# A second fold of the Fourier columns, with some moves, an order and an output tile changed

## The chip, the cores and the metric

The kernel runs on one core of a Trainium2 chip. The metric is the time of one execution on the device in microseconds (us), as the median of several runs. The engines are TensorE (PE; its weight loads appear as PEld), VectorE (DVE), ScalarE (ACT), GpSimd (POOL) and SyncE (SP), which only issues transfers (DMAs) here.

## The reference

Three stages follow each other, on 2 batches of 768 tokens. All arrays are fp32.

```
# attention: 2 batches, 8 heads, 768 tokens, 64 per head
bits   = (q @ proj > 0), (k @ proj > 0)          # 6 bits for each token
mask   = bucket(q bits) == bucket(k bits)
scores = where(mask, q @ k.T / 8, -1e9)
x      = softmax(scores) @ v                      # heads side by side: 2 x 768 x 512

# Fourier mixing over tokens and columns, then a channel MLP of width 2048
u  = x + real(fft(fft(x, axis=1), axis=2))
x  = u + relu(layernorm(u) @ w_ch1) @ w_ch2

# gated MLP: width 1024, gate mixed over tokens
h  = gelu(x @ w_in); a, v = halves of h
v  = w_sg @ (layernorm(v) * g_ln) + b_sg
out = x + (a * v) @ w_out
```

## The kernel before

Products are held to fp32 accuracy by splitting each operand into a high and a low float16 part and adding three matmuls (the pairs in `HH`: high by high, high by low, low by high); the scores of attention use fp32r parts instead. Tokens are kept in a mirrored order, so that token t and token 768 - t lie in partner tiles (tile t and tile t + 3 of the six tiles of 128 tokens).

**Attention.** For each of the 96 tiles of queries (16 heads, 6 tiles each): scores on PE, the row maximum on DVE, the exponential on ACT, a float16 split on ACT or POOL and POOL, a transpose by DMA (or, for some tiles, on PE), and the product with v on PE. `stacks` prepares a head: it makes scaled q1 and its residual k2 from one load, and then four moves of 64 partitions by 768 bring halves of q1, k1, q2, k2 where they belong; `mv` names the engine of each (S is a DMA issued by SP). Head 0 has its own list, `ENG0`. `one_hot` then writes codes into the other halves of q1 and k1.

**Fourier stage** (`fft`, once for each batch). The transform over tokens and columns is real and is folded first: rows by A + B and A - B of partner tiles (`fe`, `fo`), then columns by adding (even part) or subtracting (odd part) column c and column 512 - c. The folded parts, 257 and 256 columns wide, are split into float16 (`ee`, `oo`; the single row `oe`, `oeh`). `step1` multiplies them with the token tables (`cs`, `sn`, 385 columns) to give `yc`, `ys` and one middle row `y2`. `step2` multiplies these with the column tables (`cl`, `sl`, 257 columns), two blocks of 128 each, giving the cosine part p and the sine part q of each tile, and p - q and p + q are added to the partner tiles. `step2` runs 6 matmuls, and 2 more with `rl` where `extra` is set, 257 columns wide each, into neighbouring columns of one PSUM bank. `norm` then normalises each tile (`un`; `UN` names the engine for each batch), splits it and transposes it by DMA into `unT`.

**Channel MLP** (`ch`: lines 764 and 785 are its two products) and **gated MLP** (`gmlp`: line 881 the first product, 933 the token mixing, 984 the output product in `go`). A gated tile is turned by DMA into `gT`; `GV` lists, by count, those that take their room from the larger pool `vg` (18 buffers), the others take one of 4. `go` adds the output product to x on DVE and stores 256 KB for each of the 12 tiles.

**Order.** The two batches overlap: the second batch's attention runs beside the first batch's Fourier stage (called fft0 here) and channel MLP and beside the preparation of the weights; the second Fourier stage (fft1) runs beside the end of the first batch's channel MLP. The order in which each engine issues its instructions is made when the kernel is built, by the class `Order`: a list planner with costs for each instruction that takes, on each engine, the ready step of lowest rank. `SHIFT` adds an offset in us to the rank of named streams of work (a lower one comes earlier): w1a to w2b are weights, att1h7 is head 7 of the second batch, ch1 the second batch's channel MLP, pre1h3 the preparation that runs during head 3.

## Time and profile before

| what | value |
|---|---|
| median of 3 runs | 665.83 us (662.92 to 667.2) |
| the profiled execution | 667.98 us |
| its span, first to last instruction | 666.2 us |
| PE busy | 604.4 us of the span |
| DVE, ACT, POOL busy | 495.1, 362.2, 284.9 us |
| mean granted clock of PE | 0.967 |

The span is what the profile's rows are placed in; 1.8 us of the execution lie outside it. A row of a timeline has the start, the duration, the engine, the line of the kernel, the operation, the tile written and the tiles read. A busy time counts overlapping instructions of one engine once, and a single matmul's duration holds its latency, so the pace of matmuls is read from their starts.

### The profile page before, as it was taken

To read this page: it belongs to the slowest core of one execution; us is meant where nothing else is said; L and a number is where in the kernel's file an instruction comes from. 1 tells how busy PE (TensorE), PEld (TensorE's weight loads), DVE (VectorE), ACT (ScalarE), POOL (GpSimd) and SP (SyncE) were. 2 spreads that over 40 slices of the span, in tenths; PEclk is the share of its full clock that TensorE was granted. 3 is DMA by queue.
4 is the path that set the end of the run, shared out by engine and by line. 5 is a ranking of instruction groups with operands and counts; after the bars stand their busy time and mean duration, and the time that the engine had idled before them with its cause. 6 is when DMAs were issued, how large, how long until landed. Compare 5 with 4: busy or idle time off the path is not lost.

```text
span 666.2 us, 12742 instructions
## 1 busy us (share of the span) xinstructions
PE 604.4 (91%) x4901; PEld 412.4 (62%) x4901; DVE 495.1 (74%) x1061; ACT 362.2 (54%) x574; POOL 284.9 (43%) x246
## 2 busy tenths in 40 slices
PE   4789889847866999999999998999999999999997
PEld 3688778734755676777776647676666444444443
DVE  6897886588987866998767498669552477598883
ACT  5899999864687756675553224234352176334110
POOL 2566667594667652445424041500010004446762
PEclk9799999978968999999999999999999999999999
DMA  8999999997999999897663047942000022001335
GB/s 338 241 174 215 223 187 191 237 270 178 216 202 240 236 223 215 204 193 169 133 99 114 1 63 141 226 124 99 33 0 1 17 48 49 1 16 32 79 102 151
DMA packets 183884, 94.60 MB, mean 142 GB/s; under 512 B 166480, under 2 KB 167120, under 8 KB 183312
## 3 DMA queue, kind: packets, MB, share of 16 engines
q1 hardware_dynamic: 183392, 93.72, 64.5%
q8 instruction: 38, 0.62, 0.4%
q14 instruction: 22, 0.18, 0.1%
q10 hardware_dynamic: 432, 0.07, 0.1%
HBM read 39.31 MB, written 3.15 MB: 64 GB/s over the span
## 4 chain that ended last, share of the span: by engine, by line
PE 61%; DMA 12%; DVE 9%; ACT 7%; POOL 6%; issue 4%; SPq 1%; POOLq 0%; ACTq 0%; DVEq 0%
PE c L785 16%; PE c L764 14%; PE gi L881 9%; PE p L933 6%; DMA et<-eh 5%; PE go L984 5%; PE s L480 4%; POOL eh L347 3%; DVE nm L490 2%; PE y L635 2%; DMA k<-q 2%; DMA wide<-w 1%; DMA unT<-hl 1%; ACT e L492 1%; POOL eh L342 1%
## 5 line engine op out<-in xcount | busy, mean ns | idle before, releaser
L347 POOL TENSOR_TENSOR eh<-e,eh 128x768 f16<-128x768 f32 x80 | 138.0, 1728 | 95.9 <-ACT eh L340 93.7
L764 PE MATMUL c<-unT,w 128*128 128x256 f16 x1152 | 134.6, 273 | 4.6 <-DVE h L773 2.7
L785 PE MATMUL c<-w,h 128*128 128x512 f16 x576 | 130.9, 379 | 0.0
L764 PEld LDWEIGHTS <-w 128*128 128x128 f16 x1152 | 111.5, 98 | 25.6 <-issue 8.5
L480 PE MATMUL s<-k,q 128*128 128x384 f32 x384 | 98.5, 386 | 26.2 <-ACT e L492 15.6
L490 DVE TENSOR_REDUCE nm<-s 128x1 f32<-128x768 f32 x96 | 90.7, 949 | 22.4 <-PE s L480 20.5
L492 ACT ACTIVATE e<-s,nm 128x768 f32<-128x768 f32 x96 | 85.1, 897 | 31.2 <-DVE nm L490 20.1
L785 PEld LDWEIGHTS <-h 128*128 128x128 f16 x576 | 55.3, 98 | 59.7 <-issue 0.6
L480 PEld LDWEIGHTS s<-k,q 128*128 128x128 f32 x384 | 70.1, 208 | 33.2 <-ACT e L492 19.0
L548 PE MATMUL pav<-V,et 128*128 128x65 f16 x480 | 54.9, 198 | 12.0 <-DMA et<-eh 10.7
L772 ACT ACTIVATE h<-c 128x256 f16<-128x256 f32 x96 | 35.0, 378 | 55.4 <-PE c L764 51.8
L773 DVE SCALAR_TENSOR_TENSOR h<-c,h 128x256 f16<-128x256 f32 x96 | 39.1, 418 | 34.9 <-ACT h L772 34.8
L548 PEld LDWEIGHTS <-et 128*128 128x128 f16 x480 | 46.0, 102 | 21.5 <-DMA et<-eh 14.6
L549 PE MATMUL pav<-V,et 128*128 128x64 f16 x480 | 54.4, 196 | 0.0
L550 PE MATMUL pav<-V,et 128*128 128x65 f16 x480 | 54.3, 198 | 0.0
L881 PE MATMUL gi<-in,xT 128*128 128x512 f16 x216 | 50.5, 379 | 0.0
L881 PEld LDWEIGHTS <-xT 128*128 128x128 f16 x288 | 28.2, 98 | 34.6 <-issue 0.9
L549 PEld LDWEIGHTS <-et 128*128 128x128 f16 x480 | 46.0, 100 | 0.8
L550 PEld LDWEIGHTS <-et 128*128 128x128 f16 x480 | 46.0, 100 | 0.0
L342 POOL TENSOR_SCALAR eh<-e 128x768 f16<-128x768 f32 x32 | 30.3, 948 | 32.8 <-ACT e L492 31.0
L340 ACT ACTIVATE eh<-e 128x768 f16<-128x768 f32 x48 | 40.3, 840 | 4.2 <-DMA et<-eh 3.8
L347 POOL TENSOR_TENSOR v<-gv,v 128x512 f16<-128x512 f32 x6 | 7.3, 1238 | 57.3 <-ACT v L868 57.3
(247 smaller groups left out, 1062.6 us busy)
## 6 DMA issues: line engine op xcount, KB each, us to landing
wide<-w SPq DMA_DIRECT2D x24, 512.0 KB, 4.8
x<-qk SPq DMA_DIRECT2D x16, 384.0 KB, 4.2
k<-q SPq DMA_DIRECT2D x30, 192.0 KB, 3.8
wide<-w SPq DMA_DIRECT2D x4, 1024.0 KB, 9.3
wide<-w_in SPq DMA_DIRECT2D x16, 256.0 KB, 2.9
vst<-v SPq DMA_DIRECT2D x8, 396.0 KB, 5.0
y<-ot SPq DMA_DIRECT2D x12, 256.0 KB, 2.0
q<-q SPq DMA_DIRECT2D x15, 192.0 KB, 3.9
```

The source lines that it names most:

```text
L340: self.nc.scalar.activation(out, src, AF.Copy, scale=scale)
L347: (self.nc.vector if eng == "D" else self.nc.gpsimd).tensor_tensor(out=out, in0=a, in1=b, op=ALU.subtract)
L480: nc.tensor.matmul(s[:, hf, 0:HS], q[:, qs], k[:, hf * HS:(hf + 1) * HS], start=n == 0, stop=n == len(pairs) - 1)
L490: nc.vector.tensor_reduce(nm, x["s"], axis=AX.XY, op=ALU.max, negate=True)
L492: nc.scalar.activation(e.rearrange("p (a c) -> p a c", a=2), x["s"], AF.Exp, bias=nm)
L548: nc.tensor.matmul(pv[:, qt, 0:65], et[:, kb, :], V[:, hl, kb, 64:129], start=kb == 0, stop=False)
L549: nc.tensor.matmul(pv[:, qt, 0:64], et[:, kb, :], V[:, hl, kb, 0:64], start=False, stop=False)
L550: nc.tensor.matmul(pv[:, qt, 0:65], et[:, NT + kb, :], V[:, hl, kb, 64:129], start=False, stop=kb == NT - 1)
L764: nc.tensor.matmul(ps[:, 0:step], w1[kc][:, a, fo], uT[:, 4 * u + kc, o * P:o * P + step], start=m == 0, stop=m == 11)
L785: nc.tensor.matmul(ps, hs[n, half, f][:, a, j * P:(j + 1) * P], wv[:, w, :], start=f + m == 0, stop=f == NF - 1 and m == 2)
L881: nc.tensor.matmul(ps, xT[:, 4 * a + kc, :], w_in[kc][:, w, half * DM:(half + 1) * DM], start=n == 0, stop=n == 11)
L933: nc.tensor.matmul(ps, W[a][k][:, w, t * P:(t + 1) * P], V[v][k][:, x, :], start=n == 0, stop=n == 8)
```

## The change

The columns are folded a second time: of the 257 folded columns c, column c and column 256 - c are added and subtracted (`quarter`), because output columns of even number need only the sums and those of odd number only the differences (the other way round for the sine part). Sums and differences are written into the free half of the same tile, so the split and `step1` work on as many columns as before. `step2` then runs, for even outputs, on one block with a table of 129 columns, and for odd outputs on the other block with 128, and writes each into every second column of the PSUM tile. The number of matmuls stays, the width halves, and so do the tables `cl` and `sl`. The two fillings with zero (`oeh`, `y2`) go, because their matmuls read one row.

Head 0's four moves go to ACT, POOL, DVE, DVE in place of ACT, POOL, POOL, ACT, and the fourth reads k1's copy instead of q1. The last output tile is made, added and stored in two halves of 256 columns. `UN`, `GV`, `SHIFT` and the scale `YS` have new values.

```
 NL = DM // 2 + 1
+NE = DM // 4 + 1
 BIG = 2.0 ** 100
...
 SCALE = 1.0 / math.sqrt(D)
-YS = 2.0 ** -4
+YS = 2.0 ** -5
...
 AVL = 3
-UN = ('A', 'D')
+UN = ('D', 'A')
 LN1 = (True, False)
...
 XTB = 6
+FO = ('P', 'P')
 GOB = 2
 LO = 'PPDPDD'
-GV = (5, 8, 11)
+GV = (8, 11)
 SQ = S // 4
...
 CP = (False, False)
-ENG0 = {'hi': 'D', 'mv': 'APPA', 'oh': 'A'}
+ENG0 = {'hi': 'D', 'mv': 'APDD', 'oh': 'A'}
 W_ATT0 = 1.5
...
-    def sub(self, eng, out, a, b):
-        (self.nc.vector if eng == "D" else self.nc.gpsimd).tensor_tensor(out=out, in0=a, in1=b, op=ALU.subtract)
+    def sub(self, eng, out, a, b, op=ALU.subtract):
+        (self.nc.vector if eng == "D" else self.nc.gpsimd).tensor_tensor(out=out, in0=a, in1=b, op=op)
...
             (tk1[0:64], tq2[64:128], tq2[0:64], tk2[0:64]),
-            (tq1[64:128], tq1[0:64], tk2[0:64], tq1[64:128]),
+            (tq1[64:128], tq1[0:64], tk2[0:64], tk1[0:64] if eng is ENG0 else tq1[64:128]),
         ):
...
         sn = fp.tile([P, HT, 2, NK], F16, tag="sn", name="sn")
-        cl = fp.tile([P, 2, 2, NL], F16, tag="k1", name="cl", bufs=2)
-        sl = fp.tile([P, 2, 2, NL], F16, tag="k1", name="sl", bufs=2)
+        cl = fp.tile([P, 2, NL], F16, tag="k1", name="cl", bufs=2)
+        sl = fp.tile([P, 2, NL], F16, tag="k1", name="sl", bufs=2)
         rk = fp.tile([P, NK], F16, tag="rk", name="rk")
-        rl = fp.tile([P, NL], F16, tag="rl", name="rl")
+        rl = fp.tile([P, NE], F16, tag="rl", name="rl")
         for t, nm in ((cs, "cos_s"), (sn, "sin_s"), (cl, "cos_c"), (sl, "sin_c"), (rk, "row_k"), (rl, "row_l")):
...
         y2 = fp.tile([P, 2, NK], F16, tag="y2", name="y2")
-        nc.gpsimd.memset(oeh, 0.0)
-        nc.gpsimd.memset(y2, 0.0)
         yield 0.1
...
         oo = fp.tile([P, HT, 2, h], F16, tag="k3", name="oo", bufs=2)
-        oe = fp.tile([1, NL], F32, tag="row", name="oe")
+        oe = fp.tile([1, DM], F32, tag="row", name="oe")
+        r = h // 2
+
+        def quarter(eng, x, z):
+
+            self.sub(eng, x[:, h + 1:h + r + 1 - z], x[:, z:r], x[:, h - z:r:-1])
+            self.sub(eng, x[:, r + 1:h + 1 - z], x[:, r + 1:h + 1 - z], x[:, z:r][:, ::-1], ALU.add)
+
         for t in range(HT):
...
             nc.vector.tensor_tensor(out=e[:, 1:h], in0=e[:, 1:h], in1=e[:, DM - 1:h:-1], op=ALU.add)
-            nc.scalar.activation(ee[:, t, 0], e[:, 0:NL], AF.Copy, scale=i)
-            nc.vector.scalar_tensor_tensor(out=ee[:, t, 1], in0=e[:, 0:NL], scalar=i, in1=ee[:, t, 0], op0=ALU.mult, op1=ALU.subtract)
+            quarter("D", e, 0)
+            nc.scalar.activation(ee[:, t, 0], e[:, r:r + NL], AF.Copy, scale=i)
+            nc.vector.scalar_tensor_tensor(out=ee[:, t, 1], in0=e[:, r:r + NL], scalar=i, in1=ee[:, t, 0], op0=ALU.mult, op1=ALU.subtract)
             if t == 0:
...
                 nc.vector.tensor_copy(oe[:, h:h + 1], o[0:1, h:h + 1])
-                nc.scalar.activation(oeh[0:1, 0], oe, AF.Copy, scale=i[0:1])
-                nc.vector.scalar_tensor_tensor(out=oeh[0:1, 1], in0=oe, scalar=i[0:1], in1=oeh[0:1, 0], op0=ALU.mult, op1=ALU.subtract)
+                quarter("D", oe, 0)
+                nc.scalar.activation(oeh[0:1, 0], oe[:, r:r + NL], AF.Copy, scale=i[0:1])
+                nc.vector.scalar_tensor_tensor(out=oeh[0:1, 1], in0=oe[:, r:r + NL], scalar=i[0:1], in1=oeh[0:1, 0], op0=ALU.mult, op1=ALU.subtract)
             nc.gpsimd.tensor_tensor(out=o[:, 1:h], in0=o[:, 1:h], in1=o[:, DM - 1:h:-1], op=ALU.subtract)
-            nc.scalar.activation(oo[:, t, 0], o[:, 0:h], AF.Copy, scale=i)
-            nc.vector.scalar_tensor_tensor(out=oo[:, t, 1], in0=o[:, 0:h], scalar=i, in1=oo[:, t, 0], op0=ALU.mult, op1=ALU.subtract)
+            quarter(FO[b], o, 1)
+            nc.scalar.activation(oo[:, t, 0], o[:, r:r + h], AF.Copy, scale=i)
+            nc.vector.scalar_tensor_tensor(out=oo[:, t, 1], in0=o[:, r:r + h], scalar=i, in1=oo[:, t, 0], op0=ALU.mult, op1=ALU.subtract)
             yield 2.0
...
                 for a in range(2):
-                    nc.tensor.matmul(y[0:m, 0:NK], oeh[:, a, c0:c0 + m], rk, start=False, stop=n == last)
+                    nc.tensor.matmul(y[0:m, 0:NK], oeh[0:1, a, c0:c0 + m], rk[0:1], start=False, stop=n == last)
                     n += 1
...
         for c in range(2):
-            step1(c * P, P, ee, cs, True, yc[c])
+            step1(c * P + 1, P, ee, cs, True, yc[c])
             yield 1.9
-        step1(2 * P, 1, ee, cs, True, y2)
+        step1(0, 1, ee, cs, True, y2)
         yield 1.9
...
             p = self.pp.tile([P, 512], F32, tag="p", name="p")
-            n = 0
-            last = 5 + (2 if extra else 0)
-            for c in range(2):
+            for l in range(2):
+                n = 0
+                last = 2 + (2 if extra and not l else 0)
+                o = p[0:m, l:NL:2]
                 for a, w in HH:
-                    nc.tensor.matmul(p[0:m, 0:NL], y[c][:, a, k0:k0 + m], tab[:, c, w, :], start=n == 0, stop=n == last)
+                    nc.tensor.matmul(o, y[l][:, a, k0:k0 + m], tab[:, w, NE * l:NE + l * (NE - 1)], start=n == 0, stop=n == last)
                     n += 1
-            if extra:
-                for a in range(2):
-                    nc.tensor.matmul(p[0:m, 0:NL], y2[:, a, k0:k0 + m], rl, start=False, stop=n == last)
+                for a in range(2 if extra and not l else 0):
+                    nc.tensor.matmul(o, y2[0:1, a, k0:k0 + m], rl[0:1], start=False, stop=n == last)
                     n += 1
...
             p = step2(t * P, P, yc, cl, True)
-            q = step2(t * P, P, ys, sl, False)
+            q = step2(t * P, P, ys[::-1], sl, False)
             qdu = fp.tile([P, 3, NL], F32, tag="k3", name="qdu", bufs=2)
...
-        def go(b, t):
+        def go(b, t, parts=1):
             gT, os_ = sv.pop((b, t))
-            po = self.pc.tile([P, 512], F32, tag="go", name="go")
-            n = 0
-            for kc in range(4):
-                for a, w in HH:
-                    wv = w_out[kc // 2].rearrange("p t (k c) -> p t k c", k=2)[:, w, kc % 2, :]
-                    nc.tensor.matmul(po, gT[:, 4 * a + kc, :], wv, start=n == 0, stop=n == 11)
-                    n += 1
             ot = self.gp2.tile([P, DM], F32, tag="ot", name="ot", bufs=2)
-            nc.vector.scalar_tensor_tensor(out=ot, in0=po, scalar=os_, in1=self.XU[b][:, t], op0=ALU.mult, op1=ALU.add)
-            nc.sync.dma_start(out=self.out[b, t], in_=ot)
+            m = DM // parts
+            for j in range(parts):
+                po = self.pc.tile([P, 512], F32, tag="go", name="go")[:, 0:m]
+                c = slice(j * m, j * m + m)
+                n = 0
+                for kc in range(4):
+                    for a, w in HH:
+                        wv = w_out[kc // 2].rearrange("p t (k c) -> p t k c", k=2)[:, w, kc % 2, c]
+                        nc.tensor.matmul(po, gT[:, 4 * a + kc, :], wv, start=n == 0, stop=n == 11)
+                        n += 1
+                nc.vector.scalar_tensor_tensor(out=ot[:, c], in0=po, scalar=os_, in1=self.XU[b][:, t, c], op0=ALU.mult, op1=ALU.add)
+                nc.sync.dma_start(out=self.out[b, t, :, c], in_=ot[:, c])
...
         for x in pend:
-            go(*x)
+            go(*x, 2 if x == pend[-1] else 1)
...
     GAP = {"DVE": 0.19, "POOL": 0.13}
-    SHIFT = {"sg": 34.0, "w2a": 34.0, "fft0": -30.0, "w2b": 8.0, "out": -4.0, "fft1": -8.0, "att1h7": 4.0, "in": 4.0, "ch1": 19.0}
+    SHIFT = {"sg": 34.0, "w2a": 26.0, "fft0": -30.0, "out": -4.0, "fft1": -4.0, "att1h7": 8.0, "in": 4.0, "att1h5": 8.0, "w2b": 15.0, "ch1a": -30.0, "att1h4": 15.0, "pre1h3": -30.0}
     LOOK, OVER = 12, 0.3
...
     sn[:, [0, HS]] = 0.0
-    c = np.arange(DM // 2)
-    l = np.arange(NL)
-    a = 2 * np.pi * ((c[:, None] * l[None, :]) % DM) / DM
-    cl, sl = np.cos(a), np.sin(a)
-    sl[0] = 0.0
-    sl[:, [0, NL - 1]] = 0.0
+    c = np.arange(P)
+    le, lo = np.arange(0, NL, 2), np.arange(1, NL, 2)
+
+    def turn(f, c, l):
+        return f(2 * np.pi * ((c[:, None] * l[None, :]) % DM) / DM)
+
+    cl = np.concatenate([turn(np.cos, P - 1 - c, le), turn(np.cos, c, lo)], 1)
+    sl = np.concatenate([turn(np.sin, c, le), turn(np.sin, P - c, lo)], 1)
+    sl[0, 0:NE] = 0.0
+    sl[:, [0, NE - 1]] = 0.0
...
     rk[0] = (k % 2 == 1)
-    rl = np.zeros((P, NL), np.float16)
-    rl[0] = np.where(l % 2 == 0, 1.0, -1.0)
+    rl = np.zeros((P, NE), np.float16)
+    rl[0] = np.where(np.arange(NE) % 2 == 0, 1.0, -1.0)
     codes = np.zeros((P, 4, GH, P), np.float16)
...
     return {
-        "cos_s": lay(cs), "sin_s": lay(sn), "cos_c": lay(cl), "sin_c": lay(sl), "row_k": rk, "row_l": rl,
+        "cos_s": lay(cs), "sin_s": lay(sn), "cos_c": lay(cl)[:, 0].copy(), "sin_c": lay(sl)[:, 0].copy(), "row_k": rk, "row_l": rl,
         "codes": codes, "pops": pops, "ident": np.eye(P, dtype=np.float32),
```

## Rows read from the trace of the kernel before

**Rows 1.** The page's busy time of each engine over the whole span.

```profile
PE 604.4 (91%) x4901; PEld 412.4 (62%) x4901; DVE 495.1 (74%) x1061; ACT 362.2 (54%) x574; POOL 284.9 (43%) x246
```

**Rows 2.** Stretches: length, busy PE, PEld, DVE, ACT, POOL; granted clock, DMA share, GB/s.

```profile
0.00:16.00 16.00, 6.82 (x33) 5.25 (x34) 10.84 (x19) 9.04 (x13) 3.97 (x17) 1.00 0.85 338
133.00:167.00 34.00, 21.36 (x183) 14.02 (x183) 28.57 (x42) 19.88 (x32) 23.52 (x20) 0.80 0.95 223
167.00:216.00 49.00, 35.33 (x392) 28.56 (x392) 41.81 (x96) 37.53 (x57) 32.37 (x29) 0.79 1.09 220
...
360.00:400.00 40.00, 40.00 (x245) 23.17 (x243) 28.68 (x95) 11.56 (x26) 11.18 (x12) 1.00 0.21 34
400.00:641.00 241.00, 237.87 (x1386) 135.33 (x1385) 166.04 (x454) 89.81 (x165) 63.94 (x57) 1.00 0.27 63
641.00:666.20 25.20, 21.49 (x100) 9.54 (x98) 13.29 (x31) 1.89 (x3) 9.54 (x9) 1.00 0.47 135
```

**Rows 3.** Timeline of the first 14 us: start, duration, engine, line, operation.

```profile
5.29 1.02 DVE L354 SCALAR_TENSOR_TENSOR k<-x,qsc,q 128x768 fp32r<-128x768 f32 x1
5.35 1.65 POOL L342 TENSOR_SCALAR q<-q 64x768 fp32r<-64x768 f32 x1 [4.14 <-DVE q L344]
...
6.96 0.80 PE L446 MATMUL ct<-bits,codes 128*128 128x192 f16 x4 [0.60 <-ACT bits L400]
...
8.12 0.84 ACT L340 ACTIVATE k<-q 64x768 fp32r<-64x768 f32 x1 [1.21 <-POOL q L342]
...
9.86 0.90 ACT L370 ACTIVATE q<-ct,pops 64x768 fp32r<-64x768 f32 x1
...
11.71 5.49 PE L480 MATMUL s<-k,q 128*128 128x384 f32 x16 [3.95 <-ACT k L372]
```

**Rows 4.** Timeline of DVE in the first batch's fold.

```profile
142.25 0.41 DVE L615 TENSOR_TENSOR fe<-fe 128x255 f32<-128x255 f32 x1
...
142.65 0.67 DVE L613 TENSOR_TENSOR fe<-xu 128x512 f32<-128x512 f32 x1
```

**Rows 5.** Groups by line and shape: count, busy us, mean ns, idle before.

```profile
L773 DVE SCALAR_TENSOR_TENSOR h<-c,h 128x256 f16<-128x256 f32 x96 | 39.1, 418 | 34.9 <-ACT h L772 34.8
...
L624 POOL TENSOR_TENSOR fo<-fo 128x255 f32<-128x255 f32 x6 | 6.3, 1055 | 0.4 <-DVE oe L620 0.4
...
L615 DVE TENSOR_TENSOR fe<-fe 128x255 f32<-128x255 f32 x6 | 4.9, 813 | 0.0
L734 ACT ACTIVATE un<-xu,lnm,ln 128x512 f32<-128x512 f32 x6 | 4.8, 801 | 0.0
...
L736 DVE TENSOR_SCALAR un<-xu,mv,ln 128x512 f32<-128x512 f32 x6 | 3.5, 584 | 0.1
```

**Rows 6.** Chain of waits in the first Fourier stage: start, us, what.

```profile
135.32 0.53 POOL oeh L601
...
136.59 3.46 DVE fe L613 x2
...
157.38 2.78 PE y L635 x9
...
167.18 0.76 PE p L661 x6
```

**Rows 7.** Timeline of PE in the second Fourier stage.

```profile
377.14 0.83 PE L661 MATMUL p<-sl,ys 128*128 128x257 f16 x6
377.80 0.83 PE L661 MATMUL p<-cl,yc 128*128 128x257 f16 x6
```

**Rows 8.** Chain of waits: an attention matmul of 65 columns.

```profile
126.00 0.03 PE pav L550
```

**Rows 9.** Timeline of DVE at the end.

```profile
662.53 0.75 DVE L987 SCALAR_TENSOR_TENSOR ot<-go,os,xu 128x512 f32<-128x512 f32 x1 [1.84 <-PE go L984]
```

**Rows 10.** DMA issues by line: count, KB each, median us to landing.

```profile
y<-ot SPq DMA_DIRECT2D x12, 256.0 KB, 2.0
...
cl<-cos_c SPq DMA_DIRECT2D x2, 257.0 KB, 5.7
```

## Prediction

> **What bounds the kernel now.** I read the busy totals first: TensorE (PE) is busy 604.4 of 666.2 us, so 61.8 us of idle is all that order and latency can give back, and the rest falls only if matmuls get fewer or narrower [rows 1]. The stretches then show where that idle lies [rows 2]; subtract PE's busy time from each length. From 0 to 16 it is 9.2 us. From 133 to 216, where the first batch's Fourier stage (fft0) meets the second batch's attention, it is 12.6 + 13.7 = 26.3 us, at a granted clock of 0.80 and 0.79 (a mix of the levels 1.2 and 2.4 GHz), while VectorE (DVE) is busy 28.57 of 34 and 41.81 of 49 us. From 360 to 400, where the second Fourier stage (fft1) runs, PE has no idle at all; from 400 to 641 it has 3.1 us, in the tail 3.7. What is left, 19.5 us, lies between these, most of it in the attention before 133. So one rule for each edit: behind 216 a matmul column saved is time saved, and work added to DVE, ScalarE (ACT) or GpSimd (POOL) is covered by PE; ahead of 216 it is the other way, the latency of DVE and POOL counts and PE has room.
>
> **The start.** Head 0's first score matmul begins at 11.71 [rows 3]. Before it ACT moves one half, POOL makes two moves one after the other (the first 5.35 to 7.00), ACT the fourth move (8.12 to 8.96), then, behind a move for head 1, the two one-hots from 9.86 on, 0.9 us each. The fourth move reads the half of q1 that the first one-hot overwrites, so the one-hot must wait. After the change it reads k1's copy, and ACT has no second move. The code products end at 6.96 + 0.80 = 7.76; one-hots from 7.8 to 9.6; first score at about 9.65, which is 2.1 us earlier. The two moves on DVE start after the residual (5.29 + 1.02 = 6.31) and are shorter than it at the same 768 columns, so they end by 6.31 + 2 x 1.02 = 8.4, in time. They are queued ahead of head 1's scaling and residual on DVE, whose products are needed only after six tiles of head 0; POOL only loses work. But DVE gets up to 2 us more, and weight work behind it is pushed towards the first row maxima. I take -1.5, bounds -2.1 and 0.
>
> **Second fold, the inputs (fft0).** Each batch adds 6 DVE operations of 128 columns, 2 on one row of the odd part, and 6 on POOL of 127 columns; two POOL clears go. A clean DVE operation took 0.41 us at 255 columns and 0.67 at 512 [rows 4], so about 0.27 at 128; the same operation at 255 averaged 0.813, and POOL's 1.055, since they wait for each other there [rows 5]. So DVE pays 8 x 0.27 = 2.2 to 8 x 0.81 = 6.5, POOL 6 x 0.5 (half of 1.055) = 3.2 to 6.3, in part at the same time, and the clears come off (the first is 0.53 us of the chain, just ahead of the fold, and I put both at 1.0) [rows 6]. The chain of waits runs through DVE's fold from 136.59 up to the first Fourier matmul at 157.38 [rows 6]: none of this is hidden. I take 8 x 0.45 - 1.0 = +2.6, nearer the clean rows since narrow operations meet fewer others; bounds +0.5 and +11.8 (6.5 + 6.3 - 1.0).
>
> **Second fold, the matmuls.** The second Fourier step has 50 matmuls of 257 columns a batch (8 for the middle row, 14 for each of three tiles), and afterwards 50 of 129 or 128. Six of 257 took 377.80 - 377.14 = 0.66 us, 0.110 each [rows 7]; those of 65 columns in attention follow each other at 0.03 [rows 8]. Between the two, 129 columns give 0.057. So 50 x 0.053 = 2.7 us a batch. In fft1 PE is full, so all of it counts: -2.7. In fft0 the chain passes through these products from 167.18 with four sixes and two pairs of them, about 3.2 us, and half of that goes: -1.6, bounds -2.7 and 0.
>
> What no row shows is the place they are written to: every second column of PSUM. All matmuls in this trace write neighbouring columns. The Trainium skill, page SBUF — State Buffer, section Door 1: The DMA port swizzle, says that PSUM has lines of 8 bytes, two fp32 values, and that any access which isn't contiguous significantly slows down matmuls; a step of two columns is such an access. No run here shows it yet; it is a rival below. The page TensorE: Matmul & The Clock Gate, section Back-to-back issue gap, gives 81 ns per matmul of 128 columns with its weight load; the trace's 65-column matmuls, each with a load, run at 30 ns [rows 8], so the measurement speaks against it. By the page the saving would be 50 x 0.029 = 1.5 us a batch, and the sum 2.0 us higher (1.2 in fft1, 0.8 in fft0).
>
> **Normalisation swapped.** Batch 0's six go from ACT (0.801 us each) to DVE (0.584), batch 1's the other way [rows 5]. In 167 to 216 ACT is busy 37.53 and DVE 41.81 of 49 us [rows 2]: DVE is the fuller, yet each of the six is 0.22 us shorter. I take -0.5, bounds -1.5 and +1.5 (half of 6 x 0.584 unhidden). In fft1 the swap costs 6 x 0.22 = 1.3 us at most, hidden by PE's full queue: 0.
>
> **Fold in fft1.** The same 14 operations lie beside a PE without idle; the matmuls of the first batch's channel mixing cover them, and could be drawn forward. 0; without the cover up to +3, as in fft0.
>
> **Tail and tables.** The last output add runs from 662.53, 0.75 us for 512 columns [rows 9]; with 256 the nearest DVE row is 0.418 [rows 5], so -0.33. 256 KB took 2.0 us to land [rows 10]; half of it saves between 0 and 1.0, I take 0.3. PE's second half adds next to nothing. One more store on SP has nothing behind it. Together -0.6. The two column tables shrink from 257 KB [rows 10] to half, on a DMA system busy 0.95 in 133 to 167 [rows 2]: -0.3, bounds -1 and 0. The new scale, and loads of one row in place of 128, cost nothing: as many columns pass.
>
> **Order.** New priorities, and the fifth gated tile's transpose drawn from four buffers in place of 18: a wait there would sit on SP's queue ahead of the next transposes, with seven finished tiles pending for PE as cover (0 to +2). Priorities change no work, only idle. I take 0, bounds -7 (a quarter of the 26.3) and +4.
>
> **Sum.** -1.5 + 2.6 - 2.7 - 1.6 - 0.5 - 0.6 - 0.3 = -4.6 us. The profiled execution took 667.98, 2.15 above the median, and would come to 663.4; from the median 665.83 it is 661.
>
> **Rivals.** Strided writes cost double: if a written column takes the place of two, 129 columns need the 0.110 us of 257, both matmul terms vanish, and the time is 661 + 4.3 = 665.3. For it: the rule above; against it: nothing in the trace, either way.
> The new order is what matters: it starts attention and channel mixing so that a quarter of the 26.3 us closes, 661 - 6.6 = 654.4. For it: granted clocks of 0.8 mean that closing gaps also makes matmuls faster; against it: DVE's 84 and 85% there, which no order changes.
> Slower: DVE and POOL block each other in the fold. Each added operation then costs its blocked row and none overlap: +11.8 in place of +2.6, 670.2. The other terms give 7.2, so it ends slower than before from (7.2 + 1.0) / 14 = 0.6 us for each added operation end to end, and slower by over 1% (672.5) from 1.06, a little above the blocked means. For it: the mean of 0.813 against the clean 0.41; against it: the two engines also work side by side, and only fft0 is exposed.
> That the start doesn't move, because DVE's weight work is still ahead of the first maximum, gives 662.5 and lies within the forecast.
>
> **How the numbers follow.** Forecast 0.36, of which a quarter lies under 659.2; strided writes 0.24; order 0.28, nearly all under 659.2; blocking 0.12, two thirds over 672.5. One per cent, 6.7 us, is about what can be told from no change: three runs spread over 4.3. Faster 0.35, same 0.57, slower 0.08. The range reaches from 653 (the order rival with the start's full 2.1 and some tail) to 668 (strided writes and 2.7 more for the fold), which leaves out the blocking case and some of the luckiest orders.
>
> **What would show it.** The first score matmul near 9.65. In fft1, matmuls of 128 columns starting 0.057 apart: right; 0.110: the strided rival. DVE's fold operations of 128 columns near 0.3 or near 0.8, and the first Fourier matmul 20 us after the fold begins, or 23 or more. PE's idle in 133 to 216 against 26.3. The forecast is wrong if PE idles in fft1's stretch, or if that idle moves by more than 5 us either way.

## The result and the profile after

After the change the kernel took 669.28 us (median of 20 executions, 666.29 to 675.42), the kernel before 664.63 beside it (20 executions, 660.95 to 670.78): a ratio of 1.0071 [1.0044, 1.0098], slower by 4.65 us. I had forecast 661, faster by 4.6, with a range of 653 to 668; the time lies above the range and the sign is the other one.

The two executions with a profile stand the other way round than the medians: 667.16 us after (2.1 under its median) and 667.98 before (3.3 above the 664.63). So below no stretch of one is subtracted from the other to find the 4.65 us; the traces serve to see mechanisms, and the prices come from timed runs or, where two runs issue in the same order, from their two traces laid side by side.

The page's busy line and the stretches of the kernel after answer to [rows 1, 2]; the columns are the same, the last stretch ends with this span of 665.3 us.

```profile
PE 605.2 (91%) x4913; PEld 411.8 (62%) x4913; DVE 514.2 (77%) x1082; ACT 363.4 (55%) x573; POOL 292.4 (44%) x253
```

```profile
0.00:16.00 16.00, 7.52 (x41) 5.98 (x42) 11.86 (x22) 10.20 (x15) 5.13 (x18) 1.00 0.87 333
133.00:167.00 34.00, 24.65 (x233) 17.24 (x234) 33.22 (x53) 21.51 (x33) 25.23 (x24) 0.70 1.08 236
167.00:216.00 49.00, 34.64 (x362) 27.23 (x359) 44.31 (x90) 33.23 (x50) 32.39 (x28) 0.81 1.00 206
360.00:400.00 40.00, 37.41 (x226) 20.72 (x226) 25.83 (x86) 12.23 (x25) 10.07 (x13) 1.00 0.11 14
400.00:641.00 241.00, 239.03 (x1392) 136.07 (x1390) 172.49 (x466) 92.94 (x169) 67.90 (x59) 1.00 0.27 65
641.00:665.30 24.30, 21.14 (x110) 10.58 (x108) 11.33 (x29) 1.89 (x3) 7.71 (x8) 1.00 0.50 140
```

TensorE's total did not fall: 605.2 against 604.4, though half the columns of a hundred matmuls are gone. (The total alone proves little: single executions of the runs below lie between 598.5 and 611.8 us, 600.6 with the Fourier stage of before and 604.6 with cheaper columns.) VectorE has 19 us more (514.2 against 495.1). And in 360 to 400, where PE had no idle at all, it now has 40.00 - 37.41 = 2.6 us. These are the two places to look at.

**The matmuls.** PE's timeline in the second Fourier stage of the kernel after, the place of [rows 7]:

```profile
381.26 0.50 PE L672 MATMUL p<-cl,yc 128*128 128x128 f16 x3
381.56 0.86 PE L672 MATMUL p<-sl,ys 128*128 128x129 f16 x6
382.22 5.38 PE L795 MATMUL c<-w,h 128*128 128x512 f16 x24
```

Take the distance from the start of a group to the start of the next, not the duration printed, which has the pipeline's end in it. Six of 129 columns take 382.22 - 381.56 = 0.66 us, 0.110 each: exactly what six of 257 took before.

**The start.** Timeline of the kernel after in its first 10 us, against [rows 3]: the two one-hots on ACT and the first score.

```profile
7.96 0.89 ACT L372 ACTIVATE q<-ct,pops 64x768 fp32r<-64x768 f32 x1 [0.94 <-PE ct L448]
8.86 0.90 ACT L374 ACTIVATE k<-ct,pops 64x768 fp32r<-64x768 f32 x1
9.81 2.93 PE L482 MATMUL s<-k,q 128*128 128x384 f32 x8 [1.94 <-ACT k L374]
```

The first score begins at 9.81 and not at 11.71; I had written 9.65.

**The first batch's fold.** The fold begins at 136.46 here and at 136.59 before, so the 1.9 us of the start have gone on the way. For its end, take PE's timeline at the first and the second Fourier product, of the kernel before and of the kernel after:

```profile
153.81 0.34 PE L635 MATMUL y<-cs,ee 128*128 128x385 f16 x1 [0.86 <-DVE ee L617]
...
157.38 2.78 PE L635 MATMUL y<-cs,ee 128*128 128x385 f16 x9 [2.91 <-DVE vmx L171]
```

```profile
157.31 0.34 PE L645 MATMUL y<-cs,ee 128*128 128x385 f16 x1 [1.05 <-DVE ee L625]
...
158.01 1.65 PE L645 MATMUL y<-cs,ee 128*128 128x385 f16 x9
```

The matmul that waits for the last folded tile (x1) began 153.81 - 136.59 = 17.22 us after the fold's beginning and now begins 157.31 - 136.46 = 20.85 after it, 3.6 us later. The second product is only 0.8 us later (20.79 and 21.55), because before it waited 2.91 us for VectorE's work of another stream. My test of 20 us, or 23 and more, took 157.38 for the first Fourier matmul; it is that of the second product, and so the test can't decide. The added operations by line and shape, over both batches, with the normalisation and a reader of PSUM (count, busy us, mean ns, idle before):

```profile
L349 POOL TENSOR_TENSOR fo<-fo 128x127 f32<-128x127 f32 x12 | 7.7, 657 | 0.5
L349 DVE TENSOR_TENSOR fe<-fe 128x128 f32<-128x128 f32 x12 | 4.9, 407 | 0.0
L349 DVE TENSOR_TENSOR oe<-oe 1x128 f32<-1x128 f32 x4 | 2.6, 650 | 0.0
...
L746 DVE TENSOR_SCALAR un<-xu,mv,ln 128x512 f32<-128x512 f32 x6 | 5.9, 979 | 0.1
...
L689 DVE SCALAR_TENSOR_TENSOR qdu<-p,sx,qdu 128x257 f32<-128x257 f32 x6 | 2.9, 480 | 5.0 <-ACT qdu L688 4.2 <-PE p L672 0.6
```

**The second batch's fold.** The timeline of the kernel after around the idle of 2.92 us on PE:

```profile
355.51 2.56 POOL L349 TENSOR_TENSOR fo<-fo 128x127 f32<-128x127 f32 x3
...
358.10 0.91 ACT L635 ACTIVATE oo<-fo,ix 128x256 f16<-128x256 f32 x2 [2.88 <-POOL fo L349]
...
359.71 0.62 ACT L782 ACTIVATE h<-c 128x256 f16<-128x256 f32 x2
...
360.67 0.40 DVE L783 SCALAR_TENSOR_TENSOR h<-c,h 128x256 f16<-128x256 f32 x1
...
362.13 0.41 DVE L783 SCALAR_TENSOR_TENSOR h<-c,h 128x256 f16<-128x256 f32 x1
...
362.59 1.47 PE L774 MATMUL c<-unT,w 128*128 128x256 f16 x12 [2.92 <-DVE h L783]
```

Read it from below. PE waits for VectorE's half of a channel-mixing tile (h L783, the second of the two, done at 362.13 + 0.41 = 362.54), which is the last to read that tile out of PSUM. VectorE's half needs ScalarE's half (h L782), and ScalarE works in the order of the plan: ahead of h stand two evictions of the odd part (oo L635) and two of the even part, and the first of them waits 2.88 us for three added operations on GpSimd. The channel mixing that I had named as the fold's cover hangs on a queue in which the fold stands first.

### The profile page after: what moved, and what is told of

Same layout as the page of the kernel before. It is cut to its first block, busy times and chain, and to the rows that moved or that the text cites. A ratio compares the mean times of both kernels' runs of the same rounds, so it can differ in the third digit from the quotient of the medians.

```text
span 665.3 us, 12786 instructions
## 1 busy us (share of the span) xinstructions
PE 605.2 (91%) x4913; PEld 411.8 (62%) x4913; DVE 514.2 (77%) x1082; ACT 363.4 (55%) x573; POOL 292.4 (44%) x253
## 4 chain that ended last, share of the span: by engine, by line
PE 61%; DVE 14%; DMA 11%; ACT 7%; issue 3%; POOL 3%; SPq 0%; ACTq 0%; POOLq 0%; DVEq 0%
PE c L774 16%; PE c L795 15%; PE gi L891 9%; PE p L943 6%; PE go L998 5%; PE s L482 3%; DMA k<-q 3%; DVE nm L492 3%; DMA et<-eh 3%; ACT e L494 2%; PE y L645 2%; DMA wide<-w 2%; DMA x<-qk 2%; PE p L672 1%; DMA vst<-v 1%
## 5 line engine op out<-in xcount | busy, mean ns | idle before, releaser
L349 POOL TENSOR_TENSOR eh<-e,eh 128x768 f16<-128x768 f32 x80 | 140.3, 1759 | 86.9 <-ACT eh L342 76.3
L774 PE MATMUL c<-unT,w 128*128 128x256 f16 x1152 | 136.2, 275 | 6.7 <-DVE h L783 6.7
L774 PEld LDWEIGHTS <-w 128*128 128x128 f16 x1152 | 112.7, 99 | 28.5 <-issue 9.3
L482 PE MATMUL s<-k,q 128*128 128x384 f32 x384 | 96.7, 383 | 25.0 <-ACT e L494 11.7
L782 ACT ACTIVATE h<-c 128x256 f16<-128x256 f32 x96 | 34.9, 379 | 54.3 <-PE c L774 47.1
L783 DVE SCALAR_TENSOR_TENSOR h<-c,h 128x256 f16<-128x256 f32 x96 | 39.2, 417 | 22.1 <-ACT h L782 20.9
L344 POOL TENSOR_SCALAR eh<-e 128x768 f16<-128x768 f32 x32 | 31.8, 993 | 30.5 <-ACT e L494 30.0
L308 POOL TENSOR_TENSOR sg<-sg 128x384 f32<-128x384 f32 x3 | 3.0, 1002 | 71.5 <-ACT out L301 71.5
```

The source lines that it names most:

```text
L349: (self.nc.vector if eng == "D" else self.nc.gpsimd).tensor_tensor(out=out, in0=a, in1=b, op=op)
L482: nc.tensor.matmul(s[:, hf, 0:HS], q[:, qs], k[:, hf * HS:(hf + 1) * HS], start=n == 0, stop=n == len(pairs) - 1)
L774: nc.tensor.matmul(ps[:, 0:step], w1[kc][:, a, fo], uT[:, 4 * u + kc, o * P:o * P + step], start=m == 0, stop=m == 11)
```

## The experiments

The theories, after the result: **stride**, that a write to every second column of PSUM costs the time of both columns (+4.3 us against my sum); **fold**, that the added operations cost more than I said, in the first batch or in the second; **order**, that the new priorities and not the content made the time. A plan is computed from the operations and their costs, so most edits change the order of every engine's work. The five that don't (contig, contig_first, narrow, narrow_first, contig_narrow: each engine issues what it issued, in the same order) isolate a cost; the others also carry the difference of two plans. Each ratio below is to the kernel before, timed beside it (its medians were 664.1 to 665.2); a difference of 0.001 is 0.66 us.

**contig: the same products written side by side.**

```
-                o = p[0:m, l:NL:2]
+                o = p[0:m, NE * l:NE + l * (NE - 1)]
```

> The changed kernel, with the second Fourier step writing its even and odd halves side by side instead of into every second column (so the Fourier outputs of each row stand in another order and the output is not the reference's; work, instructions and issue order are the same). Theory A (a matmul that writes every second PSUM column takes as long as one of twice the width): pace of the 128-column matmuls 0.057 us instead of 0.110, 2.7 us less PE work in each Fourier stage, the time 2.5 to 5 us below the changed kernel, ratio to before 1.000 to 1.003. Theory B (the new order of the work costs the time): ratio stays at 1.005 to 1.009. Theory C (the added operations on VectorE and GpSimd cost it): pace and time as theory B.

Measured: 665.29 us, 1.0004 [0.9979, 1.0029]: less than the whole change by (1.0071 - 1.0004) x 664.6 = 4.4 us, or by the medians 669.28 - 665.29 = 4.0, and the intervals don't overlap. PE's timeline at the same place:

```profile
385.25 0.51 PE L672 MATMUL p<-sl,ys 128*128 128x129 f16 x6
385.59 5.34 PE L795 MATMUL c<-w,h 128*128 128x512 f16 x24
```

Six of 129 columns in 0.34 us: 0.057 each, half of 0.110. That is the pace I had worked out between 65 and 257 columns; it holds for neighbouring columns and not for every second one. The saving of 50 x 0.053 a batch is there and the step of two takes all of it. As the order is the same, the two traces can be laid side by side in the second batch: contig is 383.19 - 378.27 = 4.92 us behind the kernel after at the first of these products, 401.19 - 398.90 = 2.29 behind it at the first channel product after the last of them (PE L774), and 667.6 - 665.3 = 2.3 at the end. In this stage it gains 2.63 us, and nothing after it.

**no_fold: the new start, tail, priorities and normalisation, with the Fourier stage of before** (the functions of the fold and of the two Fourier steps are taken back; the rest is the kernel after).

```
-NE = DM // 4 + 1
-FO = ('P', 'P')
-YS = 2.0 ** -5
+YS = 2.0 ** -4
...
```

> Head 0's moves, the tail in halves, the new order values, but the Fourier stage of before. Theory A and C (the fold costs): ratio 0.994 to 0.999, since start and tail give 2 us and nothing is paid. Theory B (order): 1.003 to 1.008, as slow as the change itself but for start and tail.

Measured: 664.43 us, 1.0002 [0.9978, 1.0026]. This lies in neither of the two ranges, between them. All that isn't the fold is worth nothing that shows; by my terms it should have been -1.5 - 0.5 - 0.6 = -2.6 us (0.9961), outside the interval.

**fold_only: the fold, with the start, tail, priorities' values and normalisation of before.**

```
-UN = ('D', 'A')
+UN = ('A', 'D')
-GV = (8, 11)
+GV = (5, 8, 11)
-ENG0 = {'hi': 'D', 'mv': 'APDD', 'oh': 'A'}
+ENG0 = {'hi': 'D', 'mv': 'APPA', 'oh': 'A'}
...
```

> The second fold alone, all else as before. Theory A: step 2 saves nothing and the added operations cost 1 to 4 us, ratio 1.002 to 1.007. Theory B: 0.995 to 1.002. Theory C: 1.006 to 1.012.

Measured: 679.93 us, 1.0230 [1.0199, 1.0261], 15 us over before and above all three ranges. In the profiled executions the span is 10.8 us longer (677.0 against 666.2) while PE is busy as long (605.1 against 604.4 us), so nearly all of that is idle: 677.0 - 605.1 = 71.9 us against 61.8. The added operations alone can't make that (narrow, below). The plan made for these values is another one, and 6.0 us of the 10.1 lie in 216 to 345, between the two Fourier stages (129.00 - 118.82 = 10.2 us idle against 129.00 - 124.83 = 4.2). Which wait makes them was not followed up.

**old_order: the whole change with the old normalisation, gates and priorities.**

```
-UN = ('D', 'A')
+UN = ('A', 'D')
-GV = (8, 11)
+GV = (5, 8, 11)
-    SHIFT = {"sg": 34.0, "w2a": 26.0, "fft0": -30.0, "out": -4.0, "fft1": -4.0, "att1h7": 8.0, "in": 4.0, ...
+    SHIFT = {"sg": 34.0, "w2a": 34.0, "fft0": -30.0, "w2b": 8.0, "out": -4.0, "fft1": -8.0, "att1h7": 4.0, ...
```

> The whole change but with the old values of UN, GV and SHIFT. Theory A and C: 1.004 to 1.009, about as the change. Theory B: 0.995 to 1.001.

Measured: 672.2 us, 1.0113 [1.0076, 1.0150]. This is above both ranges. The new priorities don't make the kernel slow; the old ones with this content are, if anything, 0.4% worse, and the intervals overlap. Fold_only has the same old priorities and differs only in the start and the tail; it is 1.2% slower still, though start and tail are worth nothing that shows in no_fold: two plans of nearly the same work lie that far apart.

**true_price: the planner is told that a product with an output step of two takes twice as long**, and plans anew; the work is that of the whole change.

```
+            if i.outs[0].bass_ap.ap[-1][0] == 2:
+                x *= 2
```

> The changed kernel, where the planner reckons a matmul that writes every second column at twice its width, as the trace shows it. Theory D (the order is planned around matmuls that take longer than planned): 2 to 5 us below the changed kernel, ratio 1.000 to 1.004. Theory A (the columns cost PE time wherever they stand): no better, 1.005 to 1.010, the order being another throw of the dice.

Measured: 671.33 us, 1.0133 [1.0094, 1.0171], above both ranges. The theory that the plan suffers from the wrong price falls: with the right price it is no better.

**narrow: the added operations on 8 columns instead of 127 or 128**, the order as in the kernel after. Two lines of the planner, which keep the old widths in its costs, are left out of the edit shown.

```
-            self.sub(eng, x[:, h + 1:h + r + 1 - z], x[:, z:r], x[:, h - z:r:-1])
-            self.sub(eng, x[:, r + 1:h + 1 - z], x[:, r + 1:h + 1 - z], x[:, z:r][:, ::-1], ALU.add)
+            f = z if x is oe else r - 8
+            self.sub(eng, x[:, h + 1 + f - z:h + r + 1 - z], x[:, f:r], x[:, h - f:r:-1])
+            self.sub(eng, x[:, r + 1:h + 1 - f], x[:, r + 1:h + 1 - f], x[:, f:r][:, ::-1], ALU.add)
```

> The changed kernel with the added fold operations of the even and odd tiles done on 8 columns instead of 128 or 127 (the rest of the folded columns is missing, so the Fourier outputs are not the reference's); the planner is given the old widths, so that the issue order is the same on every engine. Theory A (what is lost is the written stride, the added operations cost little): 0 to 1.5 us below the changed kernel, ratio 1.005 to 1.007. Theory C (the added operations cost the 3 us that the saved columns would give): 2.5 to 6 us below, ratio 0.998 to 1.003.

Measured: 664.01 us, 1.0004 [0.9978, 1.0029], 4.5 us less than the whole change by the ratio (5.3 by the medians), and the intervals don't overlap. What is taken away on the engines is small: the shapes of 8 columns still cost 278 ns on DVE and 324 on POOL, against 407 and 657, which makes 12 x 0.129 + 12 x 0.333 = 5.5 us on two engines over both batches. That nearly as much comes off the end is largely the stall's doing. Narrow's timeline of ACT, and of PE's product that had waited, at the second fold:

```profile
353.35 0.91 ACT L635 ACTIVATE oo<-fo,ix 128x256 f16<-128x256 f32 x2 [0.27 <-POOL fo L349]
...
354.97 0.62 ACT L782 ACTIVATE h<-c 128x256 f16<-128x256 f32 x2
...
357.49 1.47 PE L774 MATMUL c<-unT,w 128*128 128x256 f16 x12
...
358.45 0.51 ACT L635 ACTIVATE oo<-fo,ix 128x256 f16<-128x256 f32 x1 [2.87 <-POOL fo L349]
```

ScalarE now waits 0.27 us for GpSimd instead of 2.88. The channel products that feed these h start at 352.07 here and at 354.29 in the kernel after; h follows them after 2.90 us here and after 5.42 there, so PE's next ones come in time. A later wait of ScalarE for GpSimd, 2.87 us at 358.45, stays, and PE has no idle to speak of (below): a wait counts only where the covering work stands behind it.

The order is that of the kernel after, so here too the traces can be laid side by side. The second fold's beginning, in the kernel after and in narrow:

```profile
349.25 2.37 DVE L620 TENSOR_TENSOR fe<-xu 128x512 f32<-128x512 f32 x2
```

```profile
347.03 2.37 DVE L620 TENSOR_TENSOR fe<-xu 128x512 f32<-128x512 f32 x2
```

Narrow is 2.22 us ahead there, 362.59 - 357.49 = 5.10 ahead at PE's product, and 665.3 - 660.2 = 5.1 ahead at the end: narrowing the second fold gains 2.88 us, and what comes after it neither adds nor gives back. In the first batch the two traces don't show a price. The last matmul of narrow's first Fourier product begins at 155.74 for 157.31, but the first product of `step2` begins at 168.54 in narrow and at 168.55 in the kernel after, with the folds at 136.37 and 136.46.

**contig_narrow: both edits at once.**

> Both at once: the changed kernel with even and odd outputs side by side and the added fold operations of the tiles done on 8 columns (Fourier outputs not the reference's; order of issue the same on every engine). If the two costs are separate (stride 4.0, fold operations 4.7 us), 8 to 9 us below the changed kernel, ratio 0.993 to 0.996. If both hide behind the same wait, no better than either alone, 0.998 to 1.001.

Measured: 659.98 us, 0.9926 [0.9892, 0.9961], 9.6 us less than the whole change by the ratio, a little more than the 8 to 9 that I expected for separate costs. Single costs were 4.4 and 4.5 by their ratios; together 9.6. The two costs add, neither hides behind the other, and together they are twice what the change lost. Against the kernel after, the trace gains 2.88 us at the second fold and 2.63 at the second batch's products, the same as narrow and contig do singly.

**contig_first and narrow_first: each edit in the first batch alone.**

```
-                o = p[0:m, l:NL:2]
+                o = p[0:m, l:NL:2] if b else p[0:m, NE * l:NE + l * (NE - 1)]
```

```
-            f = z if x is oe else r - 8
+            f = z if x is oe or b else r - 8
```

> The changed kernel with outputs side by side in the first batch's Fourier stage only (its outputs in another order, not the reference's; order of issue the same). Prediction's reading (PE is full behind 216, so columns count in the second stage; in the first they count by half): 1 to 2 us below the changed kernel, ratio 1.004 to 1.006. If the gain comes from the first stage, where the chain waits for these products: 3 to 4.5 us below, 1.000 to 1.003.

> The changed kernel with the added fold operations on 8 columns in the first batch's stage only (Fourier outputs of that batch not the reference's; order of issue the same). Prediction's reading (the fold is exposed in the first stage and covered in the second): the whole 4 to 5 us, ratio 0.999 to 1.002. If the second stage is as exposed: about half, 1.003 to 1.005.

Measured: contig_first 668.34 us, 1.0054 [1.0027, 1.0081]; narrow_first 667.64 us, 1.0040 [1.0009, 1.0072]. By the ratios the stride costs 1.1 us in the first batch and 3.3 in the second (by the medians 0.9 and 3.1), near the 1.6 and 2.7 of my split. The fold costs 2.1 us in the first and 2.4 in the second by the ratios, 1.6 and 3.6 by the medians. Each of these runs overlaps with the whole change on one side and with the full edit on the other, so the times alone don't show the splits. For the second batch the traces laid side by side decide: 2.6 for the stride, 2.9 for the fold. For the first batch a price is left only as what remains of 4.4 and 4.5, 1.8 and 1.6 us, and no run shows it by itself. The stretch 345 to 372, with the columns of the stretches above, in the kernel before, the kernel after, narrow_first and narrow:

```profile
345.00:372.00 27.00, 27.00 (x224) 17.85 (x223) 15.61 (x34) 7.40 (x18) 8.17 (x8) 1.00 0.28 80
```

```profile
345.00:372.00 27.00, 24.08 (x163) 14.10 (x161) 18.55 (x40) 6.83 (x17) 11.66 (x12) 1.00 0.20 59
```

```profile
345.00:372.00 27.00, 24.08 (x189) 15.23 (x187) 20.39 (x40) 8.14 (x17) 11.66 (x12) 0.94 0.27 74
```

```profile
345.00:372.00 27.00, 26.95 (x184) 15.93 (x183) 17.98 (x41) 7.44 (x19) 8.74 (x12) 1.00 0.19 60
```

PE has no idle before the change, 27.00 - 24.08 = 2.92 us where the second batch's fold is whole, and 0.05 where it is narrow. POOL's 11.66 us become 8.74; that this difference is 2.92 too is chance, for not all of POOL's work in the stretch lies ahead of the stall.

**start_only: the kernel before with the new start alone.**

```
-ENG0 = {'hi': 'D', 'mv': 'APPA', 'oh': 'A'}
+ENG0 = {'hi': 'D', 'mv': 'APDD', 'oh': 'A'}
-            (tq1[64:128], tq1[0:64], tk2[0:64], tq1[64:128]),
+            (tq1[64:128], tq1[0:64], tk2[0:64], tk1[0:64] if eng is ENG0 else tq1[64:128]),
```

> The kernel before with only head 0's moves changed. Theory E (the earlier first score reaches the end): ratio 0.996 to 0.998. Theory F (the attention that follows is held by ScalarE and the transfers, and takes the two microseconds back): 0.999 to 1.002.

Measured: 664.38 us, 1.0009 [0.9986, 1.0031], as theory F has it. The first score begins 1.64 us earlier (first fence below), and the time doesn't fall. Where the lead goes is seen in the exponentials of the scores: the groups of ACT between 12 and 45 us (count, least, median and largest ns, first and last start), of the kernel before and of start_only, and the stretch 16 to 33 of each.

```profile
10.07 4.25 PE L480 MATMUL s<-k,q 128*128 128x384 f32 x14 [1.94 <-ACT k L372]
```

```profile
L492 ACT ACTIVATE e<-s,nm x12: 887/901/910, 14.4 to 41.9; 128x768 f32<-128x768 f32 x12
```

```profile
L492 ACT ACTIVATE e<-s,nm x12: 881/898/907, 12.7 to 40.9; 128x768 f32<-128x768 f32 x12
```

```profile
16.00:33.00 17.00, 12.49 (x93) 11.25 (x93) 15.07 (x20) 14.25 (x21) 9.86 (x10) 0.80 1.05 246
```

```profile
16.00:33.00 17.00, 12.30 (x98) 10.44 (x99) 17.00 (x21) 13.97 (x19) 11.15 (x8) 0.90 1.12 250
```

The first exponential is 1.7 us earlier, the twelfth 1.0. At the first batch's fold nothing is left of it: it begins at 138.64 in start_only, 136.59 before (and 136.46 in the kernel after). In 16 to 33 VectorE was busy 15.07 of 17 us before and is busy all 17.00 now: the lead brings this stretch up against DVE, and PE does no more in it (12.30 against 12.49). That DVE's fullness is what eats the lead is an inference from these rows; no run took work off DVE there. The DMA engines are as full (a share of 1.05 before and 1.12 now), and the transfers that theory F named are a rival that no run tested.

**contig_ok: products side by side, with the reference's result kept.** The two halves have 129 columns each (the tables get a column of zeros), and the readers take them from PSUM in alternating runs.

```
-                o = p[0:m, l:NL:2]
+                o = p[0:m, NE * l:NE * l + NE]
...
-            return p
+            return p[:, 0:2 * NE].rearrange("p (l j) -> p j l", l=2)
```

> The change with the reference's result kept: even and odd outputs are written side by side (both 129 columns), and ScalarE and VectorE read them back in turn from PSUM. Theory A: as the version with other column order, ratio 0.998 to 1.004, if the readers take the two runs at full pace (0.48 us for 258 columns); if the stride costs the readers too, 24 reads of 0.48 us become 0.9 and the time 1.004 to 1.008. Theory B (the order): 1.005 to 1.010 whatever the pace.

Measured: 667.53 us, 1.0036 [1.0003, 1.0069], in theory A's range and 2.3 us under the whole change by the ratio, with a plan of its own and an interval that overlaps with the change's. One of its readers by line and shape in 360 to 400:

```profile
L693 DVE SCALAR_TENSOR_TENSOR qdu<-p,sx,qdu 128x258 f32<-128x258 f32 x3 | 1.4, 477 | 0.0
```

Reading 258 columns in alternating runs takes 477 ns, the plain 257 of the kernel after 480: what the step costs a matmul that writes, it doesn't cost VectorE that reads.

**contig_fo: contig_ok with the second batch's odd fold on VectorE.** Only the second batch's operations move. This takes GpSimd's part of the stall away.

```
-FO = ('P', 'P')
+FO = ('P', 'D')
```

> The version with both halves of the output columns side by side in PSUM (whose result is the reference's), with one value more changed: the odd part's added fold of both batches is allowed on VectorE, and in the second batch no longer on GpSimd's slow subtractions first. Stall theory: in the second batch's Fourier stage TensorE stands still for 2.9 us because GpSimd's three added subtractions (2.5 us) hold up ScalarE and then VectorE's queue; without them that stall goes and the time is about 3 us below the version that it changes, some 664 to 665 us, ratio to the kernel before 0.997 to 1.001. Rival (VectorE is the one that is short): the same operations now lengthen VectorE's own queue ahead of the channel MLP's split, the stall stays or moves, ratio 1.002 to 1.007. Rival (the new plan sets it): the order written by the planner changes with this value, and stages that the value doesn't touch move by more than the stall, either way.

Measured: 662.43 us, 0.9968 [0.9934, 1.0002], just under the range that the stall theory gave (0.997 to 1.001, 664 to 665 us): the gain is 4.5 us over contig_ok where 3 were expected. The stretch of the stall:

```profile
345.00:372.00 27.00, 26.91 (x176) 15.39 (x175) 19.52 (x46) 7.07 (x18) 7.14 (x6) 1.00 0.19 60
```

PE's idle is 0.09 us there. This version does all of the change's work and is 6.8 us under it by the ratio. Against the kernel before it is 2.1 us faster, but the interval just reaches 1, and the plan differs from contig_ok's, so that not all of the 4.5 us need be the stall's: PE has 1.4 us of idle in 372 to 400, where contig_ok has none.

## Why the prediction was wrong, by its own steps

**Second fold, the matmuls: the choice of the pace failed.** I took 0.057 us for 129 columns, between two rows for neighbouring columns, and the sum had -4.3 us from it. With a step of two the pace is 0.110, so the term is 0, and contig gets about 4 us back by undoing the step alone (2.63 of them in the second batch, for my 2.7). I had this as a rival at 0.24, with the right price (665.3) and the right test row, 0.110; the working was sound up to the point where "nothing in the trace, either way" was weighed three to two for the forecast. The Trainium skill, page SBUF — State Buffer, section Door 1: The DMA port swizzle, says that access to PSUM which isn't contiguous significantly slows down matmuls; these runs agree, and the number for a step of two fp32 columns is a factor of 1.9 (0.110 against 0.057). The other page of the Trainium skill that I weighed, TensorE: Matmul & The Clock Gate, section Back-to-back issue gap, gives 81 ns for 128 columns with a weight load; contig's 57 ns for 129 are less, as I had argued.

**Fold in fft1: the step failed that put it at 0.** I named the first batch's channel mixing as the cover. PE's queue did hold such matmuls; but each tile of them passes through ScalarE and VectorE between its two products, and there it stands behind the fold's own evictions. Three operations on GpSimd (2.56 us) held ScalarE for 2.88 and PE for 2.92. The traces of narrow and of the kernel after put the price at 2.88 us, the times of narrow_first and narrow at 2.4, near the "+3 without the cover" that I wrote beside the 0.

**The start: the mechanism was right, the step to the end failed.** The row came (9.81 for 9.65), the -1.5 us did not: the lead is 1.7 us at the first exponential of start_only, 1.0 at the twelfth, and gone at the first fold. That the start doesn't move the time was within my rivals, and only its place was other: the first score did move, and the lead was lost behind it.

**Second fold, the inputs: not contradicted, and not shown.** The operations were put at 8 x 0.45 = 3.6 us in the first batch, less 1.0 for the clears, on the ground that none of the chain is hidden. At the fold's end the traces of before and after agree (3.6 us later), but at the second product 0.8 us of it is left, so a part is hidden. The row that I took for the first Fourier matmul, 157.38, was that of the second product. Narrow_first takes 2.1 us off by the ratio, within the error, and its stubs of 8 columns keep two thirds of a DVE operation's time (278 of 407 ns) and half of a POOL one's. The means (407 ns for DVE's 128 columns) lie between the clean 0.27 and the blocked 0.81, as chosen. The blocking rival falls: the operations are busy (4.9 + 2.6 + 7.7) / 2 = 7.6 us a batch on both engines, so that even with no overlap they don't come to its 12.8 less the clears.

**The products of one row: put at nothing without a reason.** I wrote that loads of one row in place of 128 cost nothing, as many columns pass. PE's timeline of one cosine tile with its two one-row products, in the kernel before (from 377.80 in [rows 7]), after, and in contig:

```profile
378.47 0.38 PE L665 MATMUL p<-rl,y 128*128 128x257 f16 x2
378.69 1.46 PE L785 MATMUL c<-w,h 128*128 128x512 f16 x6
```

```profile
388.06 0.53 PE L672 MATMUL p<-cl,yc 128*128 128x129 f16 x3
388.52 0.39 PE L675 MATMUL p<-rl,y 1*128 1x129 f16 x2
...
389.14 5.38 PE L795 MATMUL c<-w,h 128*128 128x512 f16 x24
```

```profile
391.12 0.33 PE L672 MATMUL p<-cl,yc 128*128 128x129 f16 x3
...
391.78 5.34 PE L795 MATMUL c<-w,h 128*128 128x512 f16 x24
```

The eight matmuls take 378.69 - 377.80 = 0.89 us before and 389.14 - 388.06 = 1.08 after; in contig 0.66, where 8 x 0.057 are 0.46. The products without one-row matmuls show no such surplus, so it lies at the change from 128 rows to one and back, about 0.2 us a time. A batch has seven such places, in `step1` and `step2`; in the second, where PE is full, they come to about 1.2 us by their starts in the two traces. No run keeps the 128 rows, so the price is read and not tested.

**Normalisation, tables, tail, order.** The six on DVE average 979 ns, not 584, and are now longer than they were on ACT (801): the sign of -0.5 is doubtful, and no run isolates it, nor the tables' -0.3. In the tail the last add is the one of 256 columns:

```profile
662.18 0.48 DVE L1000 SCALAR_TENSOR_TENSOR ot<-go,os,xu 128x256 f32<-128x256 f32 x1 [0.83 <-PE go L998]
```

It takes 0.48 us for 0.75, and from its end to the end of the span it is 665.3 - 662.66 = 2.64 us, for 666.2 - 663.28 = 2.92 before: 0.55 us in all for my 0.6, too small to be seen in a time. For the order as a whole I took 0, and neither no_fold against before nor old_order against the change differs clear of noise; but the spread of plans is larger than my bounds for it (-7 and +4), as fold_only shows.

With 0 for the matmuls, 0 for the start and 2.9 for the second batch's fold, the sum becomes 2.6 + 2.9 - 0.5 - 0.6 - 0.3 = +4.1 us, and +5.3 with 1.2 for the one-row products; 4.65 [2.9, 6.5] was measured, and both sums lie within that error. What stays open is the first batch's share, and why two plans of almost the same work differ by up to 1.2%.

## What to carry to other kernels

Before counting on fewer columns, ask how they are written: a matmul that wrote every second column of PSUM took as long here as one that wrote them all, so write the halves side by side and let the reader pick them apart. "Covered by a full PE" holds only if the covering work doesn't pass through an engine queue in which the new work stands first: follow one tile of the cover through every engine it needs. A matmul cut to one row is not free either where it stands between matmuls of 128. And where a planner orders the work, test a part with an edit that leaves the order as it is, since any other edit measures the plan too.

## What the runs showed that I had not expected

The factor is whole: 129 columns at a step of two cost what 257 neighbouring columns cost, 0.110 us, with no sign of a smaller penalty in the full groups. VectorE, reading PSUM in alternating runs, pays nothing (477 against 480 ns for one column more). And a share of an engine that looks idle over a stretch (ACT was busy 6.83 of 27 us in 345 to 372) says nothing of the order in its queue: it was through this engine's queue that GpSimd held PE for 2.9 us.
